# Key projection first in the first segment, no memory update in the step that turns the maxima, and the output weights' preparation spread out

## The chip, the cores and the metric

The kernel runs on one core of a Trainium2 chip. The metric is the time on the device in microseconds, the median of several runs. Below, PE is TensorE (its weight loads are listed as PEld), DVE is VectorE, ACT is ScalarE, POOL is GpSimd, and SP is the queue from which every DMA of this kernel is issued.

## The reference

Two layers, each an attention block (A) and a gated block (B), are applied twice to x of 2048 rows by 640 columns, with the same weights in both layers. The kernel must compute this:

```python
x = x + A(_layernorm(x)); x = x + B(_layernorm(x))      # twice, same weights
# A: q, k, v = x@wq, x@wk, x@wv;  H = 32 heads of 20;  N = 4 segments of L = 512 rows
phi = lambda t: where(t > 0, t + 1.0, exp(t))
for s in range(N):
    p = softmax(qs @ ks.T * scale + causal_mask)         # inside the segment
    a_dot = p @ vs
    a_mem = (phi(qs) @ M) / (phi(qs) @ z + 1e-6)         # memory of earlier segments
    outs.append(g * a_mem + (1.0 - g) * a_dot)
    M = M + phi(ks).T @ vs;  z = z + phi(ks).sum(rows)
A = concat(outs) @ wo
# B: z = gelu(x@w_in);  z1, z2 = halves;  B = (z1 * (w_sp @ _layernorm(z2) + b_sp)) @ w_out
```

## The kernel before, in words

All float32 products are made of float16 parts: every operand is split into a high and a low half, and three products (high by high, high by low, low by high) are summed in PSUM. Splitting a tile costs a scaled copy on ACT and a fused subtraction on DVE (`split_scaled`, lines 81 and 82), or a copy on ACT and a subtraction on POOL.

A layer has three stages: the attention (`Attention`), the first half of B (`phase1b`, products named zp and yp) and the second half (`phase2`, products named ga to gd and cyp). The change touches the attention, and one priority in `phase1b`.

The attention works on 64 pairs of heads (16 in each of 4 segments), in steps numbered t from -16 to 164. Five steps treat two pairs. `run` writes PE's order out by hand: the instructions of PE stand in the order in which the code emits them. The other engines' orders are made by a scheduler, which a few `issue_after` blocks bind: `behind(DVE)` or `behind(ACT)` puts an instruction after the maxima's reduction, or after the exponential, that was issued in the same step. One step emits, in this order: fetches of later pairs' queries and keys from DRAM (`fetch`, tile qk); `by_queries` (tile mp, reduced on DVE to the maxima mxs); `by_keys` (tile es, exponentiated on ACT to P); in steps with t % 5 == 2 `maxes`, which turns the maxima by a matrix product into the tile mtp, splits them into mr on ACT and DVE, and writes them back into the queries by DMA; work that was posted for this step; the products of probabilities and values (`pvs`, tile pv); the casts of P into PH and PL (`cast`); and lastly a fill from a queue of dense work: projections of values (vps), queries (qps), keys (kps) and outputs (yps), with background work and reads of the memory (num) between them.

A unit (`unit`, five to a segment) projects one 128-column group of queries and of keys into two of the two PSUM buffers named dn, which the value projections use too. `out` then splits the projection on ACT and DVE into qhl or khl and stores it to DRAM (st), from where `fetch` reads it. For keys (except in the last segment) and for queries (except in the first) it also computes phi in place: a relu on ACT, an exponential on ACT into the same PSUM buffer, and a fused minimum and addition on DVE (tile relu, line 1142), which frees the PSUM buffer. For keys, `keys` then splits phi into phl, turns it by a DMA transpose into the tile pk, of which there is one, and posts `update`: 12 products into the tile mup. The tiles mup, mtp, num, and two small ones (wtp and wbc, in which the largest weight is turned and spread) share one PSUM buffer named ms: each waits until DVE or ACT has read the one before. In which of the five kinds of step an update may stand is the tuple UPD, 2, 3, 4 or 0 before.

In the first layer, `background` also measures the weights of wo, w_in and w_out (`other_scales`), derives their powers of two (wtp, wbc) and splits wo (woh, wol) and half of w_in (wi1h, wi1l), loaded by `Weight.behind`. In the second layer (`made` is true) it loads the split halves instead.

The changed code and what calls it:

## Time and profile before

| | us |
|---|---|
| median of 3 runs | 2235.47 (2233.04 to 2241.97) |
| the profiled execution: device time | 2232.87 |
| its span | 2231.2 |
| PE busy | 2092.0 |
| POOL, DVE, ACT busy | 1404.3, 1624.2, 1252.3 |
| DMA, mean over the span | 154 GB/s |
| mean granted clock of PE | 0.987 |

The profile is of one execution, and the median of the runs lies 2.6 us above that execution's device time. The span is the profile's own; the device time is 1.67 us more. In the profile's rows a line such as L1353 is a line of the kernel before, PEclk is the granted clock of PE as a share of full speed, and "idle before" names the instruction that ended an engine's idle time.

### The profile page before, as it was taken

The page shows a single profiled execution, that of the slowest core. Times are in us where ns is not written, and L with a number is a line of the kernel's source. Part 1 is how long each engine was busy: PE and PEld are TensorE (multiplying, and loading weights), DVE is VectorE, ACT ScalarE, POOL GpSimd, SP SyncE. Part 2 cuts the span into 40 slices and gives each one's busy share as a digit, 9 for nine tenths or more (in the row PEclk, how much of TensorE's full clock was granted, in tenths as well). Part 3 has the DMA queues.
Part 4 walks back from the last instruction along what each step waited for, and adds up shares of the span by engine and source line. Part 5 has one row for each costly group of instructions (what it writes and reads, how often), then busy time and mean ns, then how long its engine had stood idle before and what let it go on. Part 6 is the DMA issues. An engine that isn't in the chain of part 4 may idle for free.

```text
span 2231.2 us, 53044 instructions
## 1 busy us (share of the span) xinstructions
PE 2092.0 (94%) x21322; PEld 1264.7 (57%) x21322; DVE 1624.2 (73%) x2889; ACT 1252.3 (56%) x1641; POOL 1404.3 (63%) x1172
## 2 busy tenths in 40 slices
PE   6898788999899999999998999989999999999999
PEld 3554555666555555555554556656675555555555
DVE  8788778788677758888746787787875765676563
ACT  4587688788644433333325887878884433333331
POOL 3387888888645446466513888988895533564660
PEclk9999899999999999999999999999999999999999
DMA  6665556444676686676455356552456345877752
GB/s 185 157 177 141 157 150 188 109 120 126 166 195 188 180 260 191 155 189 175 132 170 129 98 128 166 127 129 75 125 137 152 98 123 175 216 181 177 166 150 83
DMA packets 537703, 342.79 MB, mean 154 GB/s; under 512 B 411600, under 2 KB 463312, under 8 KB 537456
## 3 DMA queue, kind: packets, MB, share of 16 engines
q1 hardware_dynamic: 537456, 339.39, 56.8%
q8 instruction: 167, 2.74, 0.5%
q14 instruction: 80, 0.66, 0.1%
HBM read 159.18 MB, written 92.55 MB: 113 GB/s over the span
## 4 chain that ended last, share of the span: by engine, by line
PE 67%; DVE 14%; ACT 7%; DMA 5%; issue 4%; POOL 2%; SPq 1%; DVEq 0%; ACTq 0%; POOLq 0%
PE zp L412 12%; PE ga L669 12%; PE cyp L705 7%; PE pv L1353 4%; PE qps L1110 3%; PE mp L1249 3%; PE gb L669 3%; PE vps L1051 3%; PE yps L1083 3%; PE gc L669 3%; PE gd L669 3%; DVE mxs L1313 3%; PE kps L1110 2%; PE es L1249 2%; ACT PH L1322 2%
## 5 line engine op out<-in xcount | busy, mean ns | idle before, releaser
L1324 POOL TENSOR_TENSOR PL<-P,PH 128x640 f16<-128x640 f32 x384 | 539.4, 1433 | 91.8 <-PE pv L1353 74.2
L1313 DVE TENSOR_REDUCE mxs<-mp 128x2 f32<-128x1024 f32 (+2 forms) x384 | 320.6, 862 | 135.3 <-PE mp L1240 133.7
L1287 ACT ACTIVATE P<-es,sc 128x1024 f32<-128x1024 f32 (+1 forms) x256 | 271.3, 1060 | 97.0 <-PE es L1240 92.3
L639 POOL TENSOR_TENSOR ts<-ts,wt 128x512 f32<-128x512 f32 x196 | 281.8, 1449 | 11.0
L412 PEld LDWEIGHTS <-th 128*128 128x128 f16 x1920 | 188.0, 98 | 169.3 <-issue 6.6
L1322 ACT CAST PH<-P 128x1280 f16<-128x1280 f32 x192 | 239.6, 1248 | 2.5 <-PE pv L1353 1.0
L669 PEld LDWEIGHTS <-wts 128*128 128x128 f16 x1536 | 150.7, 98 | 134.6 <-issue 6.7
L669 PE MATMUL ga<-zh,wts 128*128 128x432 f16 x768 | 212.0, 348 | 3.9 <-ACT u L736 3.9
L308 POOL TENSOR_TENSOR lnrs<-lnve,mhalf 128x1 f32<-128x1 f32 x96 | 59.7, 629 | 230.0 <-DVE lnve L307 223.7
L1324 POOL TENSOR_TENSOR PL<-Pb,PH 128x640 f16<-128x640 f32 x124 | 176.8, 1454 | 19.8 <-PE pv L1353 18.6
L412 PE MATMUL zp<-wi,th 128*128 128x432 f16 x960 | 181.2, 346 | 3.6 <-ACT z L448 3.6
L1051 PE MATMUL vps<-wvh,xt 128*128 128x320 f16 x640 | 155.5, 309 | 30.3 <-DVE relu L1142 22.1
L639 POOL TENSOR_TENSOR ts<-wt,wt 128x512 f32<-128x512 f16 x28 | 34.4, 1230 | 227.7 <-DMA wt<-wn 227.7
L669 PEld LDWEIGHTS <-wt 128*128 128x128 f16 x1152 | 112.7, 98 | 96.5
L1353 PE MATMUL pv<-vs,PH 128*128 128x41 f16 x2560 | 159.5, 183 | 8.2 <-DVE gm L1374 5.9
L705 PE MATMUL cyp<-wuh,ut 128*128 128x320 f16 (+1 forms) x896 | 163.6, 299 | 2.6 <-DMA ut<-un 1.8
L705 PEld LDWEIGHTS <-ut 128*128 128x128 f16 (+1 forms) x1344 | 131.1, 98 | 57.4 <-DMA ut<-un 3.9
L1249 PEld LDWEIGHTS <-qk 64*128 64x128 f16 (+1 forms) x2048 | 77.6, 94 | 149.4 <-issue 130.9
L1353 PE MATMUL pv<-vs,PL 128*128 128x41 f16 x2560 | 157.2, 182 | 2.2 <-POOL PL L1324 2.2
L412 PE MATMUL zp<-wi1h,th 128*128 128x432 f16 x640 | 149.8, 349 | 1.9 <-DMA th<-xnhl 1.9
L1353 PEld LDWEIGHTS <-PH 128*128 128x128 f16 x2560 | 139.4, 96 | 15.8 <-issue 5.9
L523 DVE SCALAR_TENSOR_TENSOR wn<-wr,wsc,wn 128x512 f16<-128x512 f32 x126 | 92.2, 770 | 75.5 <-ACT wn L522 75.4
(224 smaller groups left out, 5283.3 us busy)
## 6 DMA issues: line engine op xcount, KB each, us to landing
qk<-st SPq DMA_DIRECT2D x256, 120.0 KB
wr<-in_B_w_sp_dram SPq DMA_DIRECT2D x60, 512.0 KB
z<-z SPq DMA_DIRECT2D x32, 432.0 KB
cz<-z SPq DMA_DIRECT2D x32, 432.0 KB
xt<-in_A_x_dram SPq DMA_DIRECT2D x32, 320.0 KB
st<-qhl SPq DMA_DIRECT2D x40, 256.0 KB
st<-khl SPq DMA_DIRECT2D x40, 256.0 KB
x<-x SPq DMA_DIRECT2D x32, 320.0 KB
```

The source lines that it names most:

```text
L412: nc.tensor.matmul(zp[:, n, :FHH], a[:, k, :], b[:, k, c:c + FHH], start=(k == 0 and j == 0), stop=(k == KD - 1 and j == 2))
L639: nc.gpsimd.tensor_tensor(t, a, t if b == "t" else get(b), ALU.add if op == "+" else ALU.subtract)
L669: nc.tensor.matmul(ps, w[:, a, k % 4, :], z[:, k, j, :], start=start and k == 0 and i == 0, stop=k == NP - 1 and i == 2, skip_group_check= ...
L705: nc.tensor.matmul(yp[:, n, :320], a[:kn[k], k, :], b[:kn[k], k, n * 320:(n + 1) * 320], start=(k == 0 and j == 0), stop=(k == KO - 1 and ...
L1051: nc.tensor.matmul(ps, a[:, k, c], b[:, k, n * 320:(n + 1) * 320], start=(i == 0), stop=(i == 14))
L1110: nc.tensor.matmul(ps, a[:, k, c], b[:, k, :], start=(i == 0), stop=(i == 14))
L1249: nc.tensor.matmul(out[:, h, o:o + w], a[r, ac], b[r, bc], start=o == 0, stop=False, skip_group_check=True)
L1287: g.exp = nc.scalar.activation(P, E, AF.Exp, scale=g.esc)
L1313: e = nc.vector.tensor_reduce(mx[:, :, n, j], mp[:, :, o:o + w], AX.X, ALU.max)
L1322: nc.scalar.copy(PH, P[:, h])
L1324: (nc.gpsimd if h == 0 or n < self.N - self.TAIL else nc.vector).tensor_tensor(PL[:, c], P[:, h, c], PH[:, c], ALU.subtract)
L1353: nc.tensor.matmul(pv[:, i, h, :41], x[:, c:c + 128], v[:, j, h0 + h, :], start=(j == 0 and x is PH), stop=(j == i and x is PL), skip_grou ...
```

## The change

- A unit of the first segment projects its keys first and its queries second; in the other segments the order stays. The record of which projections are stored (`stacked`) follows the one that comes second.
- UPD is 3, 4 or 0: an update no longer stands in the step in which the maxima are turned.
- `keys` of a unit is put off, step by step, while the update of the unit before is still to come (`waiting`).
- The scales' last two parts, wtp and wbc, are taken out of the run of measurements at steps 5 to 40 and stand at steps 41 and 45. The loads of wo begin at step 42 instead of 46 and its splits at 48.4; the splits of wo and w_in are bound to the exponential of their step.
- In the last pair, the subtraction for PL on DVE is posted two steps later.
- The first load of `phase1b` gets a higher priority.

```diff
-        with tc.high_priority(offset=HP2):
-            a = load(0)
+        with tc.high_priority(offset=3 * HP2):
+            a = load(0)
+        with tc.high_priority(offset=HP2):
             xn = attn_out(0, *a)
...
-UPD = (2, 3, 4, 0)
+UPD = (3, 4, 0)
...
-        for nm in ("q", "k"):
+        for nm in "qk" if s else "kq":
             if nm == "k" and self.mem:
                 self.mem = False
                 yield 840
...
         def keys(ph):
+            if self.waiting:
+                self.post(1, lambda: keys(ph))
+                return
+            self.waiting = True
             hl = self.u3.tile([128, 2, L], F16, tag="hl", name="phl")
...
         assert self.pk_of == (s, m), (self.pk_of, s, m)
+        self.waiting = False
...
-        if nm == "k":
+        if nm == ("k" if s else "q"):
             self.stacked = NU * s + m
...
-        for c in (slice(0, 640), slice(640, 1280))[::-1 if n % 2 and h else 1]:
-            (nc.gpsimd if h == 0 or n < self.N - self.TAIL else nc.vector).tensor_tensor(PL[:, c], P[:, h, c], PH[:, c], ALU.subtract)
+        def low(engine):
+            for c in (slice(0, 640), slice(640, 1280))[::-1 if n % 2 and h else 1]:
+                engine.tensor_tensor(PL[:, c], P[:, h, c], PH[:, c], ALU.subtract)
+
+        if h == 0 or n < self.N - self.TAIL:
+            low(nc.gpsimd)
+        else:
+            self.post(2, lambda: low(nc.vector))
...
-                for i, _ in enumerate(other_scales(g, self.place, self.pl1, self.pm, "ms")):
+                scales = other_scales(g, self.place, self.pl1, self.pm, "ms")
+                for i, more in enumerate(scales):
+                    if not more:
+                        break
                     yield 5 + i
-            yield 45
-            yield 45.5
...
+                yield 41
+                next(scales)
+
+            def steps(it, times):
+                for t in times:
+                    with self.tc.issue_after(self.fetched.ins), self.behind(ACT):
+                        if next(it, it) is it:
+                            break
+                    yield t
...
+                it = g.wo.behind(lambda _: next(rows), D, KD)
+                yield 42
+                yield from steps(it, [42.5, 43, 43.5, 44, 45])
+                next(scales, None)
+                yield 47
+                yield from steps(it, [48.4 + 1.4 * i for i in range(99)])
+                g.wi[1].tiles(g.top[1])
+                yield from steps(g.wi[1].behind(self.place, FHH, 2), [56 + 1.9 * i for i in range(99)])
```

How it moves instructions is shown at three places; `_` and a number are a buffer's. First ACT, in the first layer near step 46, where wo is split. Before, woh stands ahead of the cast of the normed rows (xnhl), the cast PH, the value split vs, the output cast ohl and the keys' exponential:

```order
L1287 ACTIVATE P<-es,sc 128x2x512
L81 ACTIVATE woh<-wsth_4007,iv 128x640
L320 CAST xnhl<-xt 128x640
L1322 CAST PH<-P 128x1280
L1056 ACTIVATE vs_297<-vps 128x16x20
L1389 CAST ohl<-gm 128x640
L1137 ACTIVATE kps<-kps,sc 128x512
```

Now the same place has no woh:

```order
L1293 ACTIVATE P<-es,sc 128x2x512
L320 CAST xnhl<-xt 128x640
L1328 CAST PH<-P 128x1280
L1057 ACTIVATE vs_297<-vps 128x16x20
L1402 CAST ohl<-gm 128x640
L1138 ACTIVATE kps<-kps,sc 128x512
L1152 ACTIVATE phl<-relu,sc 128x512
```

The first of the five woh now comes a few steps later, directly behind the step's exponentials and ahead of mr:

```order
L1293 ACTIVATE P<-es,sc 128x2x256
L1293 ACTIVATE Pb<-es,sc 128x2x256
L81 ACTIVATE woh<-wsth_3705,iv 128x640
L1346 ACTIVATE mr<-mtp 16x128
L1328 CAST PH<-P 128x1280
```

Second PE, in the third segment, behind a turning of the maxima (the change of buffer ms). Before, the first three of an update's twelve products follow a query projection that is not yet finished:

```order
L1110 LDWEIGHTS wqh
L1110 MATMUL qps<-xt_301,wqh 128x512
L1203 LDWEIGHTS pk
L1203 MATMUL mup<-vs_297,pk 128x168
L1204 LDWEIGHTS pk
L1204 MATMUL mup<-vs_297,pk 128x8x20
L1205 LDWEIGHTS pk
L1205 MATMUL mup<-vs_297,pk 128x168
```

Now the projection is finished there, and the next step's mp follows; the update stands one step later:

```order
L1111 LDWEIGHTS wql
L1111 MATMUL qps<-xt_301,wql 128x512
L1111 LDWEIGHTS wqh
L1111 MATMUL qps<-xt_301,wqh 128x512
L1255 LDWEIGHTS qk_290
L1255 MATMUL mp<-qk_290 128x384
```

Third ACT at the start of the first layer, behind the splits of wk (wkh). Before, the first unit's query split comes first:

```order
L81 ACTIVATE wkh<-wstl_459,iv 128x640 x3
L81 ACTIVATE wkh<-wstl_460,iv 128x640 x2
L1124 ACTIVATE qhl<-qps 128x512
L1124 ACTIVATE khl<-kps 128x512
L1127 ACTIVATE relu<-kps,sc 128x512
```

Now the keys' chain comes first and the query split behind it:

```order
L252 ACTIVATE qc<-one,qrow 128x512
L1125 ACTIVATE khl<-kps 128x512
L1128 ACTIVATE relu<-kps,sc 128x512
L1138 ACTIVATE kps<-kps,sc 128x512
L1152 ACTIVATE phl<-relu,sc 128x512
L1125 ACTIVATE qhl<-qps 128x512
```

What moved there is the order of the two projections' evictions; the splits of wk stand where they stood.

More of the change, by code (lines that the diff above doesn't have):

```diff
@@ L934, in __init__ @@
         self.pv, self.sum, self.o = {}, {}, {}
-        self.mem, self.last, self.stacked = False, -1, -1
+        self.mem, self.last, self.stacked, self.waiting = False, -1, -1, False
         self.now, self.later, self.half, self.rd = None, {}, {}, set()
@@ L1495, in background @@
             if not made:
-                for i, _ in enumerate(other_scales(g, self.place, self.pl1, self.pm, "ms")):
+                scales = other_scales(g, self.place, self.pl1, self.pm, "ms")
+                for i, more in enumerate(scales):
+                    if not more:
+                        break
                     yield 5 + i
-            yield 45
-            yield 45.5
-            for j, (w, width) in enumerate(((g.wo, D), (g.wi[1], FHH))):
-                w.tiles(g.top[j])
-                if made:
-                    it = w.load(self.bg, width, "bg")
-                    times = [46 + 8 * j + 1.4 * i for i in range(99)]
-                elif j:
-                    it = w.behind(self.place, width, 2)
-                    times = [56 + 1.9 * i for i in range(99)]
-                else:
-                    parts = [g.top[1].tile([128, 2160], F32, tag=f"wi1{x}", name=f"wst{x}3")[:, :3 * D].rearrange("p (k c) -> p k c", c=D) for x in "hl"]
-                    rows = iter([parts[k // 3][:, k % 3] for k in range(KD)])
-                    it = w.behind(lambda _: next(rows), width, KD)
-                    times = [46 + i / 2 for i in range(KD)] + [49 + 1.4 * i for i in range(99)]
-                for i in range(99):
-                    with self.tc.issue_after(self.fetched.ins):
@@ L1515, in background @@
+                yield 41
[3 more added lines that the diff above has]
+                    with self.tc.issue_after(self.fetched.ins), self.behind(ACT):
                         if next(it, it) is it:
                             break
-                    yield times[i]
+                    yield t
+            g.wo.tiles(g.top[0])
+            if made:
+                yield 45.5
+                yield from steps(g.wo.load(self.bg, D, "bg"), [46 + 1.4 * i for i in range(99)])
+                g.wi[1].tiles(g.top[1])
+                yield from steps(g.wi[1].load(self.bg, FHH, "bg"), [54 + 1.4 * i for i in range(99)])
+            else:
+                parts = [g.top[1].tile([128, 2160], F32, tag=f"wi1{x}", name=f"wst{x}3")[:, :3 * D].rearrange("p (k c) -> p k c", c=D) for x in "hl"]
+                rows = iter([parts[k // 3][:, k % 3] for k in range(KD)])
+                it = g.wo.behind(lambda _: next(rows), D, KD)
[4 more added lines that the diff above has]
+                yield from steps(it, [48.4 + 1.4 * i for i in range(99)])
+                g.wi[1].tiles(g.top[1])
+                yield from steps(g.wi[1].behind(self.place, FHH, 2), [56 + 1.9 * i for i in range(99)])
```

## The prediction

> **What bounds the kernel now.** I read the page first.
>
> ```profile
> span 2231.2 us, 53044 instructions
> ...
> PE 2092.0 (94%) x21322; PEld 1264.7 (57%) x21322; DVE 1624.2 (73%) x2889; ACT 1252.3 (56%) x1641; POOL 1404.3 (63%) x1172
> ```
>
> PE is busy for 94% of the span, and the change adds and removes none of its products. What can be won is PE's idle time, 139 us, and the time in which its clock is halved. So I went on to the waits of PE over the whole span (us in total, times, longest).
>
> ```profile
> PE vps L1051 <- DVE relu L1142: 22.1, 10, 8.8
> ...
> PE mup L1203 <- DVE mr L1335: 12.9, 9, 2.4
> ...
> PE mp L1249 <- DVE mxs L1313: 7.5, 16, 0.8
> ...
> PE mp L1249 <- DVE mxs L1310: 5.0, 8, 1.6
> ```
>
> The change touches both: the first is the wait for a PSUM buffer dn until phi has been computed in it, the second is the update's wait behind the turning of the maxima, with which it shares the buffer ms; the last two are the scores' product that waits for the maxima's reduction, and part C needs them. Then I cut the two layers' attention into the same stretches of work. Columns: start and end, us, busy time and count of PE, PEld, DVE, ACT and POOL, granted clock, DMA share, GB/s.
>
> ```profile
> 195.64:264.91 69.27, 51.61 (x728) 34.20 (x728) 51.01 (x99) 45.81 (x58) 50.66 (x45) 0.88 0.49 132
> 264.91:350.84 85.93, 74.73 (x1157) 48.08 (x1151) 66.99 (x119) 70.03 (x88) 72.28 (x67) 1.00 0.57 155
> ...
> 1195.24:1311.02 115.78, 107.05 (x1638) 64.46 (x1632) 89.12 (x155) 100.53 (x125) 92.07 (x78) 1.00 0.41 105
> 1311.02:1367.34 56.32, 49.84 (x730) 33.01 (x726) 43.84 (x86) 42.42 (x54) 49.16 (x45) 0.94 0.68 166
> 1367.34:1443.55 76.21, 73.73 (x1157) 47.45 (x1151) 55.26 (x105) 64.89 (x78) 69.58 (x67) 1.00 0.52 130
> ```
>
> Layer 0 needs 69.27 us where layer 1 needs 56.32 (12.95 more), and then 85.93 against 76.21 (9.72 more). The difference in work is the weights' preparation, which only layer 0 has: it costs 22.67 us of the end, though PE does nearly nothing for it.
>
> **Part A, the scales and wo in layer 0.** Waits of PE from 204 to 240, and then the same place in order of time (start, us, engine, line, operation, idle before):
>
> ```profile
> PE vps L1051 <- DVE relu L1142: 8.8, 1, 8.8
> PE wbc L67 <- DVE gm L1188: 3.5, 1, 3.5
> PE wtp L60 <- DVE lnmv L306: 2.7, 1, 2.7
> ```
>
> ```profile
> 229.85 0.41 SPq L155 DMA_DIRECT2D wsth<-in_A_wo_dram  x1
> ...
> 233.06 0.83 ACT L81 ACTIVATE woh<-wsth,iv 128x640 f16<-128x640 f32 x1 [4.13 <-DMA wsth<-in_A_wo_dram]
> 236.51 0.66 ACT L1137 ACTIVATE kps<-kps,sc 128x512 f32<-128x512 f32 x1
> 237.20 0.69 DVE L1142 SCALAR_TENSOR_TENSOR relu<-kps,relu 128x512 f32<-128x512 f32 x1 [6.58 <-ACT kps L1137]
> 237.95 0.42 PE L1051 MATMUL vps<-wvh,xt 128*128 128x320 f16 x1 [8.84 <-DVE relu L1142]
> ```
>
> Here is the cause of the longest wait. ACT runs its queue in order, the first split of wo stands in it, and it waits 4.13 us for a load issued only 3.21 us before. The keys' exponential behind it comes at 236.51, the buffer is free at 237.9, PE has stood for 8.84 us. In the changed order the loads are issued at step 42 and the splits stand at 48.4, some 6 steps later; a step takes 2.9 us (115.78/40 in the row of layer 1), so the split comes about 18 us after the issue, where the wait above shows about 7.3 us (3.21 and 4.13) enough. The split also leaves its place ahead of that exponential. wtp and wbc stand alone at steps of their own, so that their 2.7 and 3.5 us shrink. The most there is to win is the whole 12.95. What stays is the work: DVE has 7.2 us more in this stretch (51.01 against 43.84), and I let a third of it, 2.4, reach the end, since DVE is idle for a quarter of it: −10.5. Bounds: −13 if all of it is hidden; −5 if only the wait for wo goes and the exponential stays late behind the other work ahead of it (xnhl, PH, vs and ohl).
>
> **Part B, w_in's splits behind the step's exponential.** The excess of 9.72 us has the same work behind it after the change: DVE 66.99 against 55.26, ACT 70.03 against 64.89. Only the places move. Bounds 0 and −5 (half of it); I take −2, near nothing, because DVE's 11.7 us more remain.
>
> **Part C, no update in the maxima's step.** The 9 waits of mup make 12.9 us. What comes next on PE in that step decides how much is won, as PE then goes on to the maxima's next product mp, which needs the reduction before it. Two places:
>
> ```profile
> 366.98 1.22 DVE L1313 TENSOR_REDUCE mxs<-mp 128x2 f32<-128x1024 f32 x1
> 369.81 0.24 PE L1203 MATMUL mup<-vs,pk 128*128 128x168 f16 x1 [1.96 <-DVE mr L1335]
> ...
> 403.98 1.22 DVE L1313 TENSOR_REDUCE mxs<-mp 128x2 f32<-128x1024 f32 x1
> 406.22 0.24 PE L1203 MATMUL mup<-vs,pk 128*128 128x168 f16 x1 [2.33 <-DVE mr L1335]
> ```
>
> At 406.22 mp could start when mxs ends, at 405.20: 1.0 of 2.33 us are won. At 369.81 mxs ends at 368.20: 1.6 of 1.96. Together 2.6 of 4.29, or 0.6, and of 12.9 us that is 7.7. The granted clock adds something:
>
> ```profile
> 406.67:410.08 3.41, 3.41 (x60) 2.60 (x58) 1.57 (x3) 1.68 (x3) 0.00 (x0) 0.50 0.99 106
> 1498.94:1502.35 3.41, 3.13 (x32) 2.32 (x32) 0.72 (x2) 1.38 (x2) 0.39 (x1) 0.50 0.52 116
> ...
> 1357.43 0.46 PE L1175 MATMUL num<-mst,phq 128*128 128x126 f32 x2 [1.20 <-DVE mst L1209]
> 1358.99:1362.40 3.41, 3.41 (x40) 2.29 (x40) 2.08 (x4) 1.54 (x2) 1.25 (x3) 0.50 0.95 257
> ```
>
> Two stretches of 3.41 us at half clock begin directly behind waits of mup, and each costs 1.7 us. But a wait of only 1.20 us comes shortly before a third, so a wait cut to half may bring one too. I take a quarter of the 3.4, 0.8. C is −8.5. Bounds: −16 (12.9 and 3.4, all gone) and −4 (a third of the waits, no clock), when mp waits in mup's stead.
>
> The Trainium skill, "TensorE: Matmul & The Clock Gate", section "What's actually happening", says that the clock is halved after at least one idle window of about 3.4 us. The rows above do not bear that out alone, since their idle stretches before half clock are 2.33 and 1.20 us long. By the page the clock's term would be 0 and the sum 0.8 us smaller.
>
> **Part D, keys first in the first segment.** Waits of PE in the first segment of layer 0 (40 to 153) and of layer 1 (1160 to 1270):
>
> ```profile
> PE vps L1051 <- DVE relu L1142: 6.5, 4, 2.1
> PE qps L1110 <- DVE vs L1057: 1.3, 1, 1.3
> ```
>
> ```profile
> PE vps L1051 <- DVE relu L1142: 4.1, 4, 1.6
> PE qps L1110 <- DVE vs L1057: 1.3, 1, 1.3
> ```
>
> Before, the keys' projection stands second and the values' right behind it, so that these wait for the keys' phi. With the keys first, the queries' projection lies between them, and in this segment the queries have no phi. The sum is 13.2 us. I take half, −6.6, because phi's exponential still stands in ACT's queue behind the same casts. Against it stands the start of layer 0:
>
> ```profile
> 42.40 0.59 PE L1110 MATMUL qps<-xt,wqh 128*128 128x512 f16 x2
> 48.58 2.47 DVE L82 SCALAR_TENSOR_TENSOR wkl<-wstl,iv,wkh 128x640 f16<-128x640 f32 x3
> 51.84 0.59 PE L1110 MATMUL qps<-xt,wqh 128*128 128x512 f16 x2 [0.34 <-DVE qhl L1128]
> 55.07 0.59 PE L1110 MATMUL kps<-xt,wkh 128*128 128x512 f16 x2
> ```
>
> The keys' weights are still being split there: the last low half ends at 51.05, so the keys' projection cannot end earlier than now. The first queries' projection, which begins at 42.40 and now lies under that splitting, comes behind it; one takes 3.2 us (51.84 to 55.07). So +3.2, and D is −3.4. Bounds +3.2 (nothing won) and −10 (13.2 less 3.2).
>
> Speaking against this part, the page's rule of the idle window would bear on the same place: PE would have little to do from 42.40 until wk is split, and by the page one window of half clock would follow. An estimate from the page is +1.7 in a sum that leaves it out; no run yet shows it.
>
> **The rest.** The low halves of the last steps (PL) on DVE only change places with the reduction behind them:
>
> ```profile
> 596.38 3.11 DVE L1324 TENSOR_TENSOR PL<-Pb,PH 128x640 f16<-128x640 f32 x2
> 599.41 0.49 DVE L1371 TENSOR_REDUCE pv<-pv 128x160 f32<-128x320 f32 x1
> ```
>
> The product that waits there needs work behind both, so 0; if PL is itself what is late next, +0.5 in a layer. The higher priority of the first load of the gated block leaves SP's rows as they stood: 0. On SP five issues of wo, 0.41 us each in the row above, come ahead of the fetches and transposes of four steps: 2 us over some 12, while a fetch stands about 3 steps, 8.7 us, ahead of its use. That cover hides them; without it they cost 2 us. The chain of keys, transpose and update may be put off by `waiting`; that costs nothing as long as three slots of relu suffice, and its failure is the third rival.
>
> **Sum.** A −10.5, B −2, C −8.5, D −3.4: −24.4. The profiled span goes from 2231.2 to 2206.8, its device time from 2232.87 to 2208.5; the median lies 2.6 above it, so 2211. The ends of the parts, added by squares as independent (to the slow side 5.5, 2, 4.5 and 6.6, to the fast side 2.5, 3, 7.5 and 6.6), give about −14 and −35, so this case's own range is 2200 to 2221.
>
> **The rivals.** (1) *More is won*: all of A and C, half of the excess in B, the best of D, −44, or 2191. For it speaks that layer 1 shows the stretch in 56.32 us with the same order of PE. Against it, DVE's work remains. (2) *The waits only move*: mp waits for mxs in mup's stead (C −2), the exponential is late behind xnhl, PH, vs and ohl as before (A −5), D's gain pays for its start (0): −7, or 2228. For it speaks that the same wait of vps lasts up to 1.6 us in layer 1, where no weights are split. Here the change does what it says and brings nothing. (3) *The gate stalls the units*, the slower end: put-off keys hold their relu tile, the next unit's relu on ACT waits for a slot, and the exponentials queued behind it wait with it, so that PE waits for P. Each such put-off costs up to a step, 2.9 us. Nine such blocks pay back 24.4 us (9 × 2.9 = 26), and it decides from there; with 13 of the 30 updates (15 in each layer), 13 × 2.9 is 38, less 24 gives +14, or 2249. Against it: in the changed order every split of phi stands ahead of the relu that takes its slot.
>
> **Chances.** Forecast 0.54, rival (1) 0.12, (2) 0.22, (3) 0.12. About 0.5%, 11 us, is what a measurement of this kernel can tell from no change: below 2224.3 is faster, above 2246.6 slower. Forecast and (1) fall in the first, 0.66; (2) is the same, 0.22; (3) slower, 0.12. The range, 2192 to 2234, holds the forecast and (2), and leaves out (3) and half of (1).
>
> **What would show it.** A: no wait of vps over 3 us near 237, no wait of woh's split for its load, and 58 to 61 us in the stretch that takes 69.27. B: 82 to 86 us in the next. C: mup waits for mr nowhere, and mp's waits for mxs (7.5 and 5.0 us in the whole span now) grow by no more than 5. D: vps waits for relu under 4 us in each first segment, and queries' products at 51 to 55 in layer 0. The prediction is wrong if layer 1, which has only C and D's second half, wins nothing, or if ACT's relu waits for a slot.

## The result, and the profile after

| | before | after |
|---|---|---|
| median, us (6 runs each) | 2234.03 | 2218.45 |
| ratio of the times, 95% interval | | 0.9932 (0.9913 to 0.9952) |
| span of the profiled execution, us | 2231.2 | 2215.5 |

The change makes the kernel 15.6 us faster, 0.7%. The forecast was 24.4, and the rival *the waits only move* had 7: the result lies about midway between the two. The page after reads:

```profile
span 2215.5 us, 53079 instructions
...
PE 2087.8 (94%) x21322; PEld 1265.2 (57%) x21322; DVE 1625.6 (73%) x2889; ACT 1250.9 (56%) x1641; POOL 1402.7 (63%) x1172
```

The work is the same; PE's idle time fell from 139 to 128 us. Waits of PE over the whole span, after (us in total, times, longest):

```profile
PE mp L1255 <- DVE mxs L1319: 14.0, 24, 1.3
PE vps L1052 <- DVE relu L1143: 13.0, 7, 4.9
...
PE num L1180 <- DVE lnmv L306: 8.3, 4, 2.7
PE num L1180 <- DVE mst L1215: 5.6, 8, 1.2
...
PE mp L1255 <- DVE mxs L1316: 2.6, 4, 0.7
```

The row of mup behind mr (12.9 us before) is gone. But the scores' product mp waits 4.1 us more for its reductions (14.0 and 2.6 against 7.5 and 5.0), and the memory's read num, which waited 6.4 us before (4.9 and 1.5), now waits 13.9. What the update no longer waits, these two products wait in its stead. The wait of vps for relu fell from 22.1 to 13.0.

Now the stretches of the attention, cut at the same turnings of the maxima as in the prediction; the third one, the end of the third segment, is where part C was priced. Layer 0, then layer 1, after:

```profile
196.42:257.55 61.13, 50.89 (x729) 33.69 (x729) 48.10 (x101) 45.11 (x57) 49.62 (x45) 0.92 0.58 150
257.55:339.58 82.03, 74.12 (x1156) 47.59 (x1150) 67.81 (x117) 70.56 (x89) 73.88 (x67) 1.00 0.59 161
339.58:411.60 72.02, 63.71 (x956) 43.52 (x950) 58.62 (x115) 55.72 (x70) 59.50 (x53) 0.95 0.60 155
1294.98:1350.15 55.17, 48.45 (x731) 32.38 (x726) 44.15 (x88) 42.55 (x54) 49.49 (x46) 0.97 0.70 170
1350.15:1427.37 77.22, 73.81 (x1156) 47.44 (x1150) 56.19 (x105) 64.87 (x78) 69.44 (x67) 1.00 0.49 128
1427.37:1498.18 70.81, 62.48 (x956) 42.46 (x950) 58.63 (x115) 55.72 (x70) 60.15 (x53) 0.98 0.52 114
```

The third stretch took these times before:

```profile
350.84:421.25 70.41, 63.25 (x957) 42.39 (x951) 59.53 (x115) 55.87 (x70) 60.90 (x53) 0.95 0.59 157
1443.55:1514.30 70.75, 63.35 (x957) 42.66 (x951) 59.36 (x115) 55.96 (x70) 60.52 (x53) 0.95 0.48 115
```

So in layer 0 the first stretch wins 8.1 us (69.27 before) and the second 3.9 (85.93). The third loses 1.6 in layer 0 and gains nothing in layer 1. There the prediction had the larger share of part C's 8.5 us (the three waits of mup in each layer's third stretch make 10.1 of the 12.9).

The first stretch of layer 0 is three cycles from one turning of the maxima to the next. In the first of them PE treats the scales (wtp and wbc), in the second stands the wait of vps. These two, before and then after:

```profile
195.64:221.39 25.75, 18.13 (x242) 11.32 (x242) 19.62 (x47) 15.89 (x20) 15.50 (x15) 0.93 0.34 89
221.39:245.99 24.60, 15.76 (x236) 9.98 (x231) 14.87 (x30) 17.97 (x23) 17.68 (x16) 0.79 0.72 190
```

```profile
196.42:218.43 22.01, 18.03 (x239) 10.95 (x239) 16.95 (x40) 15.69 (x20) 15.64 (x15) 0.92 0.63 166
218.43:240.03 21.60, 16.54 (x238) 10.63 (x232) 15.76 (x37) 14.58 (x18) 17.60 (x17) 0.84 0.62 154
```

Of the 8.1 us, 3.7 lie in the cycle of the scales, 3.0 in that of the long wait, and the last 1.4 in the third cycle, whose granted clock went from 0.91 to 1.00.

The whole account of the two profiled executions, from the start of each product:

| stretch | before, us | after, us | difference |
|---|---|---|---|
| start to the sixth turning of the maxima in layer 0 (first segment) | 146.84 | 147.62 | +0.8 |
| from there to the last turning of layer 0 | 426.00 | 415.60 | −10.4 |
| to the first value projection of layer 1 (mostly the gated block) | 573.24 | 570.65 | −2.6 |
| to the sixth turning in layer 1 (first segment) | 118.91 | 115.06 | −3.9 |
| to the last turning of layer 1 | 400.79 | 400.78 | 0.0 |
| to the end | 565.38 | 565.75 | +0.4 |

The 2.6 us of the gated block are no effect that I can name: kernels below, which have the changed kernel's work there, took 569 to 575 us.

### The profile page after: what moved, and what is told of

Its sections match the earlier page's. It is cut to its first block, busy times and chain, and to the rows that moved or that the text cites. A ratio compares the mean times of both kernels' runs of the same rounds, so it can differ in the third digit from the quotient of the medians.

```text
span 2215.5 us, 53079 instructions
## 1 busy us (share of the span) xinstructions
PE 2087.8 (94%) x21322; PEld 1265.2 (57%) x21322; DVE 1625.6 (73%) x2889; ACT 1250.9 (56%) x1641; POOL 1402.7 (63%) x1172
## 4 chain that ended last, share of the span: by engine, by line
PE 67%; DVE 14%; ACT 7%; issue 4%; DMA 4%; POOL 3%; SPq 1%; ACTq 0%; DVEq 0%; POOLq 0%
PE ga L670 12%; PE zp L412 11%; PE cyp L706 7%; PE pv L1366 4%; PE qps L1111 4%; PE vps L1052 3%; PE gb L670 3%; PE mp L1255 3%; PE yps L1084 3%; DVE mxs L1319 3%; PE gc L670 3%; PE gd L670 3%; PE kps L1111 2%; PE es L1255 2%; ACT PH L1328 2%
## 5 line engine op out<-in xcount | busy, mean ns | idle before, releaser
L1332 POOL TENSOR_TENSOR PL<-Pb,PH 128x640 f16<-128x640 f32 x124 | 175.8, 1447 | 20.3 <-PE pv L1366 19.3
```

What stands on the lines that cost most here:

```text
L1332: engine.tensor_tensor(PL[:, c], P[:, h, c], PH[:, c], ALU.subtract)
```

## The experiments

Each kernel is the changed one with an edit or two. The times are medians beside runs of the kernel before on the same chip; the ratio is to that. A ratio's interval reaches 3 to 5 us to either side, so two rows are apart for certain from about 5 us on (an estimate from these intervals). What is smaller rests on the traces, one execution of each kernel.

| kernel | median, us | ratio (95%) |
|---|---|---|
| upd_back: updates in the maxima's step again | 2218.85 | 0.9936 (0.9923 to 0.9950) |
| queries_first: queries first everywhere | 2222.67 | 0.9952 (0.9937 to 0.9967) |
| bg_back: preparation of the weights as before | 2229.00 | 0.9989 (0.9977 to 1.0001) |
| read_later: third unit's reads a step later | 2215.09 | 0.9918 (0.9903 to 0.9933) |
| dve_light: no normalisation in segments 2 to 4 | 2218.32 | 0.9937 (0.9916 to 0.9959) |
| dve_light_upd: the same, updates as in upd_back | 2207.19 | 0.9882 (0.9867 to 0.9897) |
| unbound: splits not bound behind the exponential | 2225.52 | 0.9961 (0.9947 to 0.9975) |
| load_late: wo loaded from step 45.5 | 2219.40 | 0.9929 (0.9916 to 0.9942) |
| kf1_read: read_later, keys first in layer 1 alone | 2213.40 | 0.9913 (0.9899 to 0.9928) |
| kf1_read_upd: the same, updates as in upd_back | 2220.03 | 0.9942 (0.9928 to 0.9957) |
| kf1_norm_act_upd: normalisation on ACT, keys first in layer 1 alone, updates as in upd_back | 2234.72 | 1.0007 (0.9996 to 1.0018) |
| kf1_reads_all: all reads a step later | 2232.16 | 0.9990 (0.9976 to 1.0003) |

### The update's place undone (upd_back)

```diff
-UPD = (3, 4, 0)
+UPD = (2, 3, 4, 0)
```

> The changed kernel, but an update may again stand in the step that turns the maxima (UPD 2, 3, 4, 0); everything else of the change stays. Theory 1 (the prediction's part C): the nine waits of mup behind the maxima's turning come back and the kernel is about 8.5 us slower than the changed one, near 2227. Theory 2 (from the trace after): what C won at the end of the third segment, it paid back at once, since one update moved to just ahead of a read of the memory that needs it; per layer the three cycles around it (19.29, 17.22 and 18.68 us before; 16.56, 23.95 and 16.29 after, in layer 0) sum to +1.6 and +0.1 us. Then the kernel is 0 to 3 us faster than the changed one, 2215 to 2218, these cycles go back to 19.3, 17.2 and 18.7 us, and the wait of num for the memory of 2.65 us in each layer is gone.

2218.85 us, within 1 us of theory 2's 2215 to 2218 and far from 2227: in the changed kernel part C is not apart from nothing, and the 8.5 us of the forecast are ruled out. The wait of mup came back, but not everywhere where the prediction had counted it. Waits of PE, whole span:

```profile
PE mup L1209 <- DVE mr L1348: 11.7, 7, 2.4
```

Seven waits, not nine. Those of the first segment (1.71 us in layer 0 and 0.81 in layer 1 before) do not return, since with the keys first the update falls into another step anyway: the prediction counted these 2.5 us in C, and D's edit removes them without C. For the 11.7 us that mup waits here, other products wait less than in the changed kernel: num 6.0 us (7.9 against 13.9), vps for relu 3.0 (10.0 against 13.0) and mp for mxs 2.3 (14.3 against 16.6). As only the update's place differs, this is the exchange that C made. The three cycles around the moved update sum to 57.0 us in layer 0 (56.8 after) and 54.0 in layer 1 (55.6 after); the one of 23.95 us went back to 17.1 as expected, and the first of the three in layer 0 took 21.1 us where 19.3 were expected.

### Where C's gain went: the read behind the update (read_later)

This is the changed kernel in that cycle: PE and DVE in order of time (start, us, engine, line, operation, idle before).

```profile
378.56 0.24 PE L1209 MATMUL mup<-vs,pk 128*128 128x168 f16 x1
379.42 0.24 PE L1211 MATMUL mup<-vs,pk 128*128 128x168 f16 x1
```

```profile
380.56 1.23 DVE L1316 TENSOR_REDUCE mxs<-mp 128x4 f32<-128x1024 f32 x1 [2.07 <-PE mp L1246]
381.70 0.88 DVE L305 BATCH_NORM_STATS2 lnst<-xt 128x6 f32<-128x320 f32 x2
382.49 0.73 DVE L1153 SCALAR_TENSOR_TENSOR phl<-relu,sc,phl 128x512 f16<-128x512 f32 x1
383.15 0.48 DVE L1058 SCALAR_TENSOR_TENSOR vs<-vps,vs 128x320 f16<-128x320 f32 x1
383.55 0.32 DVE L1215 TENSOR_TENSOR mst<-mup,bmask 128x168 f32<-128x168 f32 x1
```

```profile
384.01 0.55 PE L1180 MATMUL num<-mst,phq 128*128 128x126 f32 x1 [2.65 <-DVE lnmv L306]
```

mup is done at 379.66, and its sum mst, the memory itself, only starts at 383.55: it is posted one step later, behind that step's maxima (mxs, which first waits 2.07 us for PE), and four other operations stand before it. The read num, written in that very step, needs mst. The row names lnmv, but lnmv ends at 383.99 and is of another tile; the memory that num reads is mst, done at 383.87. Before, the update stood one step earlier (388.06) and its read 6.1 us behind it (394.15), without a wait; now PE comes to the read 2.8 us behind the update's start and stands for 2.65. In layer 0 these idle microseconds have a second price:

```profile
384.01:387.42 3.41, 3.41 (x16) 3.41 (x16) 0.15 (x1) 0.00 (x0) 0.98 (x2) 0.50 0.44 90
```

The read's sixteen products ran at half clock and took 3.6 us in place of 1.9. In layer 1 they ran at full speed (1.9 us) behind the same wait; there a stretch of half clock came earlier, directly behind the wait of vps for relu (2.0 us):

```profile
1465.56:1468.97 3.41, 3.41 (x21) 2.71 (x19) 0.66 (x3) 1.32 (x2) 3.41 (x3) 0.50 1.16 153
```

Four other kernels (queries_first, bg_back, unbound, load_late) have the same update and the same read. In all ten places, two to a kernel, this cycle holds one or two stretches of 3.41 us at half clock; it took 22.6 to 22.7 us with one and 23.8 to 24.1 with two. So I moved the read.

```diff
-RD = (-6, -1, 9, 14, 24)
+RD = (-6, -1, 10, 14, 24)
```

> The changed kernel, but the reads of the memory for the third unit stand one step later (offset 10 in place of 9). Theory 2: the updates moved out of the maxima's step left only about 5 us between the product mup and the read that needs it, and the DVE's queue lets the sum (mst) out 3.9 us after mup's end; one step later it is there. The wait of 2.65 us and the half clock behind it go in both layers (the cycle of 23.95 us in layer 0 and 22.74 in layer 1 falls to about 18 and 17), and the two waits of 1.2 us in the second segment go: 10 to 12 us faster than the changed one, near 2207. Rival: the read does not wait for that update but for other work on DVE, and only moves its wait along: within 3 us of the changed one.

2215.09 us, 3.4 less than the changed kernel, which the times alone cannot tell from nothing; expected were 10 to 12. The wait of 2.65 us is gone in both layers:

```profile
PE num L1180 <- DVE mst L1215: 3.2, 6, 0.8
PE num L1180 <- DVE lnmv L306: 3.0, 2, 1.5
```

The third stretch fell to 69.24 us in layer 0 (72.02 after) and to 67.67 in layer 1 (70.81): 2.8 and 3.1, not 5 to 6. A second wait of that cycle stayed (vps for relu, 2.0 us in both layers), and PE now waits there for mxs (0.5 us) and with the maxima's turning (1.1 us). Each layer won back one stretch of half clock: layer 0 keeps one of two (3.41 us of 6.83), layer 1 has none. Elsewhere a cycle of the fourth segment lost 0.6 us in each layer, one of layer 1's second segment 2.0, and one of layer 0's first segment, where nothing was edited, 1.6 by a stretch of half clock. So theory 2 has the right cause and a size two to three times too large.

### Is C worth anything once the read is out of its way? (kf1_read, kf1_read_upd)

```diff
-        for nm in "qk" if s else "kq":
+        for nm in "kq" if s == 0 and self.g.wo.made else "qk":
...
-RD = (-6, -1, 9, 14, 24)
+RD = (-6, -1, 10, 14, 24)
```

> The changed kernel with two edits far apart in time: keys first only in layer 1 (layer 0 projects its queries first again), and the reads of the memory for the third unit one step later. Theory 1, part D: keys first costs layer 0 2.8 us at its start and gives back about half in the first segment; so the first turning of the maxima in layer 0 comes 2.8 us earlier than after, some 1.5 us stay to the end, and layer 1 keeps its gain. With the 3.4 us that the later read alone won: near 2213.5. Rival: layer 0's start is covered by work behind it, and the kernel stays where the later read alone stands, 2215.

> As kf1_read, but an update may again stand in the step that turns the maxima. Theory 2: once no read stands right behind the moved update, taking the update out of that step is worth something, 1.5 to 3 us in the end of the third segment in each layer: this kernel is 3 to 6 us slower than kf1_read, near 2218. Rival: the update's place is worth nothing whatever the read does, because PE then waits for the next result of DVE: within 2 us of kf1_read.

2213.40 and 2220.03 us, of the same chip: 6.6 us for C, a little over what was expected (3 to 6), though the two intervals just touch; the two profiled executions are 3.8 us apart. The third stretch gives 70.13 and 69.54 us with the updates in the maxima's step, 69.24 and 67.66 without: 2.8 us. Another 3.6 lie in two cycles of layer 0's first segment, and not all of that is C. With queries first the update's wait is back in one of them (1.7 us, where kf1_read waits 1.0 for mxs). But each of the two also holds a stretch of half clock that kf1_read doesn't have, and the one in the other cycle, worth 1.6 us, stands behind a wait of vps (2.1 us) that both kernels have. So C's mechanism holds once the read is later, its size lies nearer to 3 to 5 us by the traces, and its worth depends on what stands behind the update.

kf1_read is also the test of D in layer 0: the first turning of the maxima comes at 74.75 us, against 77.79 after, and start to sixth turning takes 144.98 us, against 147.62. It is the fastest of the full kernels, 0.9913 of the kernel before, but that lies inside the interval of the later read alone.

### Is DVE's queue the limit? (dve_light, dve_light_upd, kf1_norm_act_upd)

The chain of waits of the changed kernel runs through DVE in this stretch, so I took its normalisation away from all rows but those of the first segment.

```diff
-            nc.vector.tensor_scalar(xt, xt, mv[:, 0:1], rs, ALU.subtract, ALU.mult)
+            if t < 4:
+                nc.vector.tensor_scalar(xt, xt, mv[:, 0:1], rs, ALU.subtract, ALU.mult)
```

> The changed kernel without the normalisation (subtraction of the mean and scaling by the deviation, one DVE operation of 1.2 to 1.9 us a tile) of the rows of the second to fourth segment, so that its output is not the reference's; its statistics are still computed. Meant to be compared with the next kernel. Theory 3: in the second half of the third segment (the three cycles that take 56.8 and 55.6 us after) the chain runs through DVE's queue, so that taking the update out of the maxima's step only moves PE's wait to the next result of DVE. With DVE relieved these three cycles fall to 50 to 53 us. Rival: DVE is not what holds them, and they stay at 55 to 57.

> As dve_light (no normalisation in the second to fourth segment), but an update may stand in the step that turns the maxima again. Theory 3: with DVE relieved, the waits of mup behind the maxima's turning are no longer hidden under DVE's chain, and this kernel is 5 to 9 us slower than dve_light, the prediction's part C coming back. Rival (theory 2, the late read of the memory alone): the read's wait after the moved update is as long with the lighter DVE, and both kernels agree within 2 us.

2218.32 and 2207.19 us. My theory 3 fell: the lighter DVE did nothing for the changed kernel (71.29 and 69.62 us in the third stretch), and with it the update's place as before is 11 us *faster*, not slower. Of both layers the third stretch falls to 65.20 and 64.22 us when the updates stand as before. Waits of PE in dve_light, and one row of its DVE:

```profile
PE num L1181 <- DVE lnmv L306: 11.5, 4, 4.2
```

```profile
382.82 2.31 DVE L1154 SCALAR_TENSOR_TENSOR phl<-relu,sc,phl 128x512 f16<-128x512 f32 x1
```

The read's wait grew to 4.2 us in each layer, although DVE had less to do, because one of the operations in front of mst took 2.31 us in place of 0.73. So the read is what holds the changed kernel there; the pair shows it, as one edit lies between the two. That DVE's load holds it where the read doesn't is less sure. It rests on the same stretch in upd_back (72.2 and 69.2 us) against dve_light_upd. Leaving the operation out takes load off DVE, but also a link out of the chain from the rows' statistics to their splits, and no run parts the two. The lighter DVE with the later read was not tried.

Moving the normalisation to ACT, to keep what it computes, was meant to harvest this.

```diff
+                nb = g.small.tile([128, 1], F32, tag="lnnb", name="lnnb")
+                nc.vector.scalar_tensor_tensor(nb, mv[:, 0:1], -1.0, rs, ALU.mult, ALU.mult)
+                nc.scalar.activation(xt, xt, AF.Identity, bias=nb, scale=rs)
```

> Keys first only in layer 1, reads as in the changed kernel, updates allowed in the maxima's step, and the normalisation of the rows of the second to fourth segment on ACT (scale and bias) in place of DVE. Leaving that operation out made the kernel with such updates about 11 us faster than its counterpart (2207.2 against 2218.9). Theory 3, as the two lighter kernels left it: DVE's queue sets the end of the third segment when the updates stand as before, so relieving it wins there; ACT has room (about 0.8 us a tile): 2205 to 2211. Rival: the operation sits as badly in ACT's queue, ahead of exponentials that PE waits for, and the gain is lost: 2215 to 2222.

2234.72 us, the time of the kernel before, and worse than the rival said. The third stretch took 70.41 and 74.31 us, far from 65.20 and 64.22. The edit hardly relieved DVE. Its new operation lnnb, one number per row, took nearly as long as the normalisation. Here are the groups of DVE in the third stretch of layer 0 (busy us, mean ns), upd_back's first:

```profile
L1033 DVE TENSOR_SCALAR xt<-xt,lnmv,lnrs 128x640 f32<-128x640 f32 x4 | 5.0, 1260 | 0.0
```

```profile
L1037 DVE SCALAR_TENSOR_TENSOR lnnb<-lnmv,lnrs 128x1 f32<-128x1 f32 x4 | 3.8, 955 | 0.0
```

DVE is busy for 58.1 us there, against 59.5 in upd_back and 53.0 in dve_light_upd, and ACT for 58.8 against 56.0. So this kernel added work to ACT and took little from DVE, and it does not test theory 3. A part of the loss, some 4 us, lies in the gated block (574.59 us against 570.37 in kf1_read_upd), where nothing was edited; that stays open.

### The weights' preparation (bg_back, unbound, load_late)

bg_back has the background work of the kernel before (its lines stand in the diff above).

> The changed kernel with the weights' preparation of the kernel before (loads of wo from step 46, the two small products wtp and wbc within the run of the scales, splits not bound behind the exponential). Theory 1 (parts A and B): about 12 us slower than the changed one, near 2230; in layer 0 the stretch that takes 61.1 us after goes back to about 68 and the next from 82.0 to about 86; the wait of vps for relu of 8.8 us returns. Rival: most of it came from the updates moved out of these stretches, and the kernel is at most 5 us slower than the changed one.

2229.00 us, 10.5 more than the changed kernel, as expected; the stretches go back to 68.96 and 85.34 us. ACT and PE of bg_back, in the place of the 8.84-us wait:

```profile
235.05 0.83 ACT L81 ACTIVATE woh<-wsth,iv 128x640 f16<-128x640 f32 x1 [3.13 <-DMA wsth<-in_A_wo_dram]
238.50 0.66 ACT L1138 ACTIVATE kps<-kps,sc 128x512 f32<-128x512 f32 x1
239.94 0.42 PE L1052 MATMUL vps<-wvh,xt 128*128 128x320 f16 x1 [7.85 <-DVE relu L1143]
```

Inside the first stretch the loss is not at this wait, though. Its cycle takes 23.3 us, 1.7 more than after; the cycle of the scales takes 27.9, 5.9 more, with PE at half clock for 13.7 us:

```profile
196.47:224.36 27.89, 21.82 (x241) 13.63 (x241) 19.44 (x48) 15.91 (x20) 16.07 (x15) 0.76 0.33 89
```

Two edits take the load and the place of wo's split apart. Neither touches the scales.

```diff
-                    with self.tc.issue_after(self.fetched.ins), self.behind(ACT):
+                    with self.tc.issue_after(self.fetched.ins):
```

> The changed kernel, but the splits of wo and w_in in layer 0 are not bound behind the exponential of their step. Theory 1: the binding is what part B won in the stretch of 82.0 us in layer 0: it goes back to 85 to 86, and the kernel is 3 to 4 us slower than the changed one; the stretch before it, 61.1 us, stays within 1 us, since the loads are early. Rival: the stretch of 82.0 us owes its gain to the earlier end of wo's preparation, and the binding does nothing: within 1 us in both stretches.

```diff
-                yield 42
-                yield from steps(it, [42.5, 43, 43.5, 44, 45])
+                yield 45
                 next(scales, None)
-                yield 47
-                yield from steps(it, [48.4 + 1.4 * i for i in range(99)])
+                yield 45.5
+                yield from steps(it, [46, 46.5, 47, 47.5, 48])
+                yield from steps(it, [49 + 1.4 * i for i in range(99)])
```

> The changed kernel, but wo is loaded from step 45.5 as before and split from step 48 on; the two small products wtp and wbc stand at 41 and 45 and the splits stay bound behind the exponential. Theory 1 (the prediction's reading of the wait of 8.84 us): the late load is what held ACT, and with it the wait of vps for relu goes from 4.9 back to about 8.8 us, the stretch of 61.1 us to about 65. Rival: it was the split's place ahead of the keys' exponential that held it; bound behind the exponential, a late load costs nothing there: the stretch stays at 60 to 62.5 us.

load_late stays at 2219.40 us, its stretch at 62.44, and the wait of vps is 5.14 us, near the value of the changed kernel (4.90) and not 8.8. The 1.3 us of the stretch (61.13 after) are not apart from nothing: it takes 60.4 to 62.8 us in upd_back, queries_first, read_later, kf1_read and kf1_read_upd, which prepare wo as the changed kernel does. So the late load alone costs nothing that shows: once the split stands behind the exponential, ACT does not meet it too early. unbound is 7.1 us slower, and not where I had expected it: the stretch of 61.13 us grows to 66.84, the next from 82.03 to 84.29 (81.7 to 83.9 in those five). Waits of PE and of ACT in that first stretch, unbound:

```profile
PE vps L1052 <- DVE relu L1143: 5.1, 1, 5.1
PE es L1255 <- ACT P L1293: 3.0, 1, 3.0
```

```profile
ACT woh L81 <- DVE iv L74: 2.5, 1, 2.5
```

With the early load the wait of vps shrinks without the binding too. But the split then meets ACT before its scale (iv) is there, ACT stands for 2.5 us, and PE waits 3.0 us for the probabilities (P) behind it. So with the binding the split comes without a wait at either time of the load. How much of part A it is worth is not shown: without it the cycle of the long wait takes 25.9 us, more than the 24.6 before. And the cycle of the scales stays won in both kernels (22.2 and 22.0 us, 25.75 before).

### Keys first (queries_first)

> The changed kernel, but units of the first segment project their queries first again. Theory 1 (the prediction's part D, sharpened by the trace after): keys first lost about 0.8 us at the start of layer 0 and won about 4.5 us at the start of layer 1, so undoing it costs 3 to 4 us: near 2222. Rival: the gain of layer 1's start has another cause (a transfer or the gated block before it), and the kernel stays at 2218; then the first product of the scores in layer 1 stands as far behind the first value projection as after (35.2 us), not as before (36.6 us).

```diff
-        for nm in "qk" if s else "kq":
+        for nm in "qk":
```

2222.67 us, 4.2 more than the changed kernel: the size that was expected, but within what two rows can tell apart. The two profiled executions are 4.2 us apart too, and only 0.6 of that lies in the first segments: 3.0 for keys first in layer 1, less 2.4 against it in layer 0. Another 1.1 lies in the rest of layer 0 and 2.4 in the rest of layer 1, where D edits nothing. The first score product of layer 1 stands 36.3 us behind the first value projection (36.6 before, 35.2 after). That row decides nothing, as the same distance is 34.9 to 36.7 us in the other kernels with keys first there and the normalisation on DVE.

### All reads a step later (kf1_reads_all)

```diff
-RD = (-6, -1, 10, 14, 24)
+RD = (-5, 0, 10, 15, 25)
```

> As kf1_read (keys first only in layer 1, the third unit's reads one step later), but the reads of all five units one step later. Theory 2 said of all reads: PE waits where a read stands in the same step as the DVE operation that completes its memory. The eight waits of num that are left in kf1_read (6.2 us in all: 0.49, 1.52, 0.38 and 0.76 us in each layer) go, and the kernel is 3 to 6 us faster than kf1_read (2213.4): 2207 to 2210. Rival: the waits are in stretches that something else holds, or the moved reads push updates into worse places: within 2 us of kf1_read, or slower.

2232.16 us, 18.8 more than kf1_read: a miss. All waits of num are gone, and this came in their place (whole span; the second row is kf1_read's):

```profile
PE mtp L1344 <- DVE gm L1193: 23.5, 23, 3.4
```

```profile
PE mtp L1344 <- DVE gm L1193: 4.0, 5, 1.1
```

gm is the operation that empties the read's product from the buffer ms; the maxima's turning mtp stands two steps behind the moved reads and needs the same buffer. It is the wait of mup behind mtp turned round: five kinds of product share one buffer, and each move of one of them is paid by its new neighbour.

## Why the prediction was right, and where its terms were not

The direction and range held. The range, 2192 to 2234, was wide enough for a kernel in which the whole of C failed. The parts, by the prediction's own steps:

| part | predicted, us | measured, us | by |
|---|---|---|---|
| A, scales and wo | −10.5 | about −8 | stretch 69.27 to 61.13; 68.96 in bg_back |
| B, w_in's splits | −2 | about −3 | stretch 85.93 to 82.03; 85.34 in bg_back |
| A and B | −12.5 | −10.5 | bg_back |
| C, the update's step | −8.5 | −0.4, not apart from 0 | upd_back |
| D, keys first | −3.4 | −4.2, not apart from 0 | queries_first |
| the rest | 0 | not apart from 0 | −15.6 less the others |

**Part C is the step that failed.** It said that 0.6 of the nine waits, 7.7 us, would be won because the next product mp can start as soon as mxs ends. It looked one product ahead. Two things were not in it. First, an update put off by a step comes nearer to the read that needs its memory: num waits 2.65 us in both layers and in layer 0 then runs 1.7 us longer at half clock, and another wait of that cycle (vps for relu, 2.0 us) is new too; together that eats the gain of the update's three waits there (4.9 us in layer 0). That is shown by upd_back, where the waits go back to mup, by the third stretch of read_later (2.8 and 3.1 us shorter), and by the pair kf1_read and kf1_read_upd, where C is worth something again (2.8 us in the third stretch). The order of PE after, which was there to read, has that read a few rows behind the moved update. Second, two waits of the first segment (2.5 us) were counted in C, though D's edit removes them alone. The bound of −4 that the prediction gave C was not low enough. Rival (2), *the waits only move*, was right for this part: the sum of mp's and num's waits grew by 11.6 us (4.1 and 7.5), against 12.9 that went. Its place was not the one named: mp took a third, num the rest.

**Part A came out near its size, and less than half of it at the wait that was put first.** The prediction led with the wait of 8.84 us, by the late load *and* the split's place ahead of the exponential, and named the waits of wtp and wbc (2.7 and 3.5 us) beside it without a price of their own. The cycle of the long wait won 3.0 us of the stretch's 8.1, the cycle of the scales 3.7. In that one PE is idle for 4.0 us where it was 7.6; wtp now waits 1.0 us, wbc not, and the read num 1.5 in their place. No run parts the scales from the rest, so that this share is argued from the rows. Of the load and the split's place, load_late shows that the load may be late if the split is bound; unbound shows that an early load without the binding is worse by 5.7 us in this stretch. A late load without the binding, with the scales as changed, was not tried. The remaining vps wait of 4.9 us is the one for which the prediction gave its lower bound: the exponential behind xnhl, PH, vs and ohl.

**Part B** came out somewhat larger than its −2. Without the binding 2.3 us of it go (84.29 in unbound), but 84.29 is only 0.4 us above the highest of the five kernels named there, so that the binding as its cause is likely and not shown.

**Part D was right in sum by luck, with both of its terms off and its size open.** Half of the waits, 6.6 of 13.2 us, were to be won and 3.2 lost at the start of layer 0. Nearly all of these waits went, and some others came. Waits of PE in the first segment of layer 0 (40 to 153) and of layer 1 (1148 to 1254), after:

```profile
PE vps L1052 <- DMA o<-ohl: 1.3, 1, 1.3
...
PE vps L1052 <- DVE relu L1143: 0.2, 1, 0.2
```

```profile
PE vps L1052 <- DVE qhl L1129: 2.2, 1, 2.2
PE vps L1052 <- DVE relu L1143: 1.1, 2, 0.9
```

Layer 1 won 3.9 us in the profiled execution, more than its half (2.7). There the sign is sure: its first segment took 118.9 us before and 118.1 in queries_first, and 112.6 to 117.2 in all nine kernels that project keys first there and normalise on DVE. Layer 0 was to win 0.7 net and lost. It lost 2.0 to 2.8 us at its first turning (77.79, against 75.82 before and 75.02 in queries_first) and won 0.4 to 1.2 us of that back up to the sixth turning. Its start, after:

```profile
45.84 1.03 PE L1111 MATMUL kps<-xt,wkh 128*128 128x512 f16 x2 [3.14 <-ACT wkh L81]
51.76 0.63 PE L1111 MATMUL kps<-xt,wkl 128*128 128x512 f16 x1
52.96 0.59 PE L1111 MATMUL qps<-xt,wqh 128*128 128x512 f16 x2
...
56.96 0.38 PE L1111 MATMUL kps<-xt,wkl 128*128 128x512 f16 x1
```

```profile
45.84:49.25 3.41, 2.34 (x6) 0.60 (x7) 3.41 (x9) 2.82 (x4) 0.00 (x0) 0.50 0.13 51
49.25:52.66 3.41, 3.41 (x10) 1.22 (x9) 2.45 (x7) 0.72 (x1) 0.00 (x0) 0.53 0.00 0
```

The queries' projection stands behind the keys', at 52.96, as forecast. The keys' projection itself ran at half clock for two stretches of 3.41 us: one product takes 0.63 us there and 0.38 later. The idle stretch ahead of it is 3.14 us. This comes with keys first: all eight kernels that project keys first in layer 0 have 6.8 us or more of half clock at this place, five of the six others have none, and kf1_norm_act_upd has 3.4.

The Trainium skill, "TensorE: Matmul & The Clock Gate", section "What's actually happening", says that an idle window of about 3.4 us halves the clock until a window has been busy. The prediction kept this rule out of its sum and priced it at 1.7 us at this place. The trace agrees in kind, behind 3.14 us of idle time, but the half clock lasted two such windows.

At num 2.65 us of idle time were followed by half clock in layer 0 and not in layer 1. Two things show in the traces of the fourteen kernels. Within an execution all changes of the clock lie a whole number of steps of 3.41 us apart, so the same wait can fall into one step or be cut by the border of two. And no step at full speed was followed by half clock with PE idle for less than 1.2 us (35%) of it, while some with PE idle for more than half of theirs were not followed by it. So idle time alone does not decide, and the rest stays open.

**The third rival**, that put-off updates stall the units, did not come: no wait of ACT's relu for a slot stands among PE's or ACT's waits.

**What would show it**, as the prediction listed it: the stretch of 58 to 61 us was 61.1, the next 82 to 86 was 82.0, vps waited for relu 0.2 and 1.1 us in the first segments (under 4 was asked), mup waits for mr nowhere, mp's waits grew by 4.1 where at most 5 were allowed. Two signs failed: vps still waits 4.9 us near 230 (none over 3 was expected), and the list had no entry for num, where C's gain went.

## What to carry to other kernels

When an instruction is moved out of a wait, look not at what can start next but at who needs its result, and how many steps nearer that reader now stands: here a read in the step of its own input's last operation took back the whole gain in its stretch. Do the same for the buffer it shares, since each product moved gets a new neighbour there (all reads a step later: 19 us). And count a wait once: two parts of one change that both remove it do not add up. Before naming the cause of a stretch's gain, cut the stretch finer: here nearly half of part A lay one cycle away from the wait that explained it.

## What the runs showed of the hardware that I had not expected

The low half of phi (phl) is one DVE operation with both inputs in SBUF, 128 by 512. Here it is in two kernels at the same place in layer 1, with POOL beside it. After, DVE and POOL:

```profile
1230.24 4.21 DVE L1153 SCALAR_TENSOR_TENSOR phl<-relu,sc,phl 128x512 f16<-128x512 f32 x1
```

```profile
1225.69 8.21 POOL L1332 TENSOR_TENSOR PL<-P,PH 128x640 f16<-128x640 f32 x6
```

read_later, DVE and POOL:

```profile
1232.01 1.49 DVE L1153 SCALAR_TENSOR_TENSOR phl<-relu,sc,phl 128x512 f16<-128x512 f32 x1
```

```profile
1227.47 8.64 POOL L1332 TENSOR_TENSOR PL<-P,PH 128x640 f16<-128x640 f32 x6
```

In both it began 4.5 us into POOL's run of six subtractions. In the first case it ended 0.5 us behind that run; in the second it got through in 1.49 us while the run went on. Over the thirty of them the time goes from 0.70 to 4.21 us in the kernel after, while the same kind of operation with one input in PSUM (khl) takes 0.68 in the mean of forty. The cycle that holds it took 16.92 us after and 14.49 in read_later, so which of the two happens is worth 2.4 us, as much as some of the edits tried here. The long one, 4.2 us, also stands at this place in upd_back and unbound, the short one, 1.5, in bg_back, load_late and kf1_read. Behind each of the long ones PE waits 2.2 us for the next split on DVE, and behind none of the short ones. After:

```profile
1235.11 0.30 PE L1052 MATMUL vps<-wvh,xt 128*128 128x320 f16 x1 [2.19 <-DVE qhl L1129]
```

So the changed kernel lost these 2.4 us in layer 1's first segment, against part D. What decides it is finer than these rows show. An operation of 2.3 us at this line lengthened the wait of num in dve_light, beside POOL's subtractions too.

The Trainium skill, "SBUF — State Buffer", section "Who interferes with whom", says that a DVE instruction with two SBUF inputs contends with a GpSimd instruction that reads SBUF. The rows agree: phl spreads, and khl stays between 0.67 and 0.69 us in all forty. That one such operation can be held through several of POOL's is how these rows read; no run takes POOL's work away to show it.
